# GpSimd drains between experts, result rows scaled on one engine, and the fallback path placed out of line

## Chip, cores and metric

One core of a Trainium2 chip runs the kernel. The metric is the device time of one execution in microseconds (us), as the median of several executions. A profiled execution of the same program gives the rows below; its span is the time from its first to its last instruction.

The engines are TensorE (PE; PEld is its weight load), VectorE (DVE), ScalarE (ACT), GpSimd (POOL) and SyncE (SP). In the rows a name with a q behind it (POOLq, ACTq, PEldq) is the sequencer of that engine: branches, drains, semaphore waits and register loads, which the profile does not count as busy time.

## The reference

A gated linear attention (a state per head that decays by a gate and takes in k times v) gives 3072 rows of 384 numbers. A mixture of 8 experts follows: every row goes to one expert, chosen by the largest gate logit, and comes back scaled.

```python
for t in range(S):                       # S = 768, head_dim 48, 4 x 8 heads
    state = f[:, :, t, :, None] * state + np.einsum('bhd,bhe->bhde', k[:, :, t], v[:, :, t])
    y[:, :, t] = np.einsum('bhd,bhde->bhe', q[:, :, t], state)
...
x = np.ascontiguousarray(attn_out.transpose(0, 2, 1, 3)).reshape(B * S, H * D)
...
e_idx = np.argmax(logits, axis=1)
for e in range(E):                       # E = 8, D = 384, F = 1024
    mask = e_idx == e
    h = np.maximum(x[mask] @ w1[e], 0.0)
    ye = h @ w2[e]
    out[mask] = gate_w[mask, None] * eom[mask, e, None] * ye
```

## The kernel before

The kernel is a program for the Tile framework, fully unrolled. Its first part, until about 127 us of the span, is the attention, in 24 tiles of 128 positions; each tile's rows are scattered by an indirect DMA that POOL issues (line 339, 24 of them) into a DRAM buffer sorted by expert. The second part, `Experts.run`, takes the experts `s` = 0 to 7 in the order of their load; `CAPS` is the number of rows that each may hold (512, 448, 432, 416, 400, 400, 384, 376). Every fp32 product is made of three products of rounded halves (`wh`/`wl`, `hh`/`hl`, `xh`/`xl`).

One expert runs as follows. `mm1` (line 760) makes the hidden tiles `h_ps`, ACT and DVE turn them into `hh` and `hl`. For experts with four row tiles (`s` 0 to 5), `mm2` (line 782) makes the result transposed; `y_out` copies it, and in the next expert's `mm1` stage `put` transposes it back, ACT scales it by the gate (line 820, 384 columns at once) and `scatter` (line 825) sends it to the output rows. For the last two experts (`s` 6 and 7, three row tiles) `mm2_rows` (line 796) makes result rows directly in PSUM: for each row tile, ACT scales the left 192 columns (line 801), DVE the right 192 (line 803), and `scatter` follows.

`scatter` is an indirect DMA that POOL issues. It writes rows of `out`, and each waits for the landing of the one ahead of it, since they write the same tensor. The tile `o` that it reads has three buffers. Apart from the scatters, POOL does only one small conversion per expert in this part (`dst`, line 687).

The order on DVE, ACT, POOL and PE is the order of the code: `chain` fixes it after recording. SP issues the loads of the weights and of the experts' rows, and waits only for free buffers.

At the end, every engine loads a flag (line 1085). If it is set (line 1090), the `general_path` recomputes everything in loops that hold for any input. With these inputs it never is. The program is a list of blocks: the main block, which ends in a conditional branch on each engine; the blocks of the general path; a short block for the case that the flag is not set, in which each engine waits for its own last work; and the end block, in which SP waits for all DMAs, every engine drains and all meet at a barrier, the semaphores are cleared, and all meet once more (rows of line 1130).

Of the kernel before, what the change touches and what calls it, by code (L numbers as in the profile page):

```python
# [13 lines left out]
AF = mybir.ActivationFunctionType  # L14
ALU = mybir.AluOpType
# [5 lines left out]
N, DM, E, F = B * S, H * D, 8, 1024  # L21
# [555 lines left out]
class Experts:  # L577
# [208 lines left out]
    def mm2_rows(self, s, step):  # L786

        k, nc = self.k, self.nc
        for j, n in self.rows(s):
            ps = self.psy.tile([128, 512], F32, name=f"y_ps{j}")  # L790
            i = 0
            for f in range(KF):
                wh, wl = self.whl[2, s, f // 2]
                hh, hl = (t[:, j * TS:j * TS + n] for t in self.hs[s, f][0])
                for a, b in ((hh, wh), (hl, wh), (hh, wl)):
                    nc.tensor.matmul(ps[0:n, 0:DM], a, b[:, f % 2, :], start=(i == 0), stop=(i == 3 * KF - 1))  # L796
                    i += 1
                step(j * KF + f)
            t = self.yp.tile([TS, DM], F32, name="o", bufs=3)
            half = DM // 2  # L800
            nc.scalar.activation(out=t[0:n, 0:half], in_=ps[0:n, 0:half], func=AF.Copy,
                                 scale=k.gain[0:n, j, s:s + 1])
            nc.vector.tensor_scalar(out=t[0:n, half:DM], in0=ps[0:n, half:DM], scalar1=k.gain[0:n, j, s:s + 1],
                                    scalar2=None, op0=ALU.mult)
            self.scatter(s, j, n, t)

    def y_out(self, s):
# [52 lines left out]
    def step(self, n):  # L860
        for _ in range(min(n, len(self.todo))):
            self.todo.pop(0)()

    def run(self):
        step = self.step
        step(len(self.todo))
        self.load_rest(1)
        for f in range(AHEAD):
            if f == AHEAD - 2:
                self.x_late()  # L870
            self.mm2(0, f)
        for s in range(E):
            if s > 0 and s + 1 < E:
                self.load(s + 1, self.k.number[0:1, s + 1:s + 2])
            back = self.rows(s - 1) if s > 0 and len(self.rows(s - 1)) > KC else []
            if s == 0:
                later = self.meta.pop()
                self.gains()
                self.meta = [later]
            for f in range(KF):  # L880
                self.mm1(s, f)
                if s == 0:
                    self.gain(2)
                    if f in (3, 5):
                        self.split(1, 1, f // 2 - 1)
                if f % 2 == 0 and (2, s, f // 2) in self.wr:
                    self.split(2, s, f // 2, self.nc.gpsimd if s == 0 else None)
                if 1 <= f <= len(back):
                    self.put(s - 1, *back[f - 1])
            front = [lambda i=i: self.split(1, s + 1, i) for i in range(KF // 2)  # L890
                     if (1, s + 1, i) in self.wr]
            for c in range(KC):
                front.insert(2 * c + 2 if s > 0 else 2 * c + 1, lambda c=c: self.x_in(s + 1, c))
            if s + 1 == E:
                front = []
            self.gain(len(self.gq))
            self.gains()
            if len(self.rows(s)) <= KC:
                self.mm2_rows(s, lambda i: self.gain(1) if i % 3 != 1 else front.pop(0)() if front else None)
                self.gain(len(self.gq))  # L900
                continue
            for f in range(KF):
                for part in range(len(self.hs[s, f])):
                    if not (s == 0 and part == 0 and f < AHEAD):
                        self.mm2(s, f, part)
                if front:
                    front.pop(0)()
                self.gain(2)
                if s == 1:
                    step(1)  # L910
            self.gain(len(self.gq))
            self.y_out(s)
            if s == 0:
                self.todo += check(self.nc, self.k, self.r, self.kp, self.pso)


def check(nc, k, r, pool, psum):


    ok = pool.tile([128, NTC * NP], F32, name="ok")  # L920
    okc = pool.tile([128, 1], F32, name="okc")
    okb = pool.tile([128, 1], BF16, name="okb")
    bad = pool.tile([128, 1 + 2 * E], F32, name="bad")
    k.bad = pool.tile([128, 1], I32, name="badi")

    def count():
        ps = psum.tile([128, KC, 128], F32, name="o_ps")[:, 0, 0:1]
        nc.tensor.matmul(ps, k.ones, okb, start=True, stop=True)
        nc.vector.tensor_scalar(out=bad[:, 0:1], in0=ps, scalar1=float(128 * NTC * NP), scalar2=None, op0=ALU.is_lt)

    def verdict():
        with nc.allow_low_precision(reason="a count of at most 17"):
            nc.vector.tensor_reduce(out=k.bad, in_=bad, axis=AX.X, op=ALU.add)

    return [
        lambda: nc.vector.tensor_scalar(out=ok, in0=r.pend, scalar1=PMIN, scalar2=None,
                                        op0=ALU.is_ge),
        lambda: nc.vector.tensor_reduce(out=okc, in_=ok, axis=AX.X, op=ALU.add),
        lambda: nc.vector.tensor_copy(out=okb, in_=okc),
        lambda: nc.vector.tensor_tensor(out=bad[:, 1:1 + E], in0=k.tokens, in1=k.caps, op=ALU.is_gt),  # L940
        lambda: nc.vector.tensor_scalar(out=bad[:, 1 + E:1 + 2 * E], in0=k.tokens, scalar1=float(HELD), scalar2=None,
                                        op0=ALU.is_lt),
        count,
        verdict,
    ]
# [107 lines left out]
def chain(tc, nc, engines, start=0):  # L1053

    last = {}
    for i in list(nc.cur_bb.bb.instructions)[start:]:
        if i.engine in engines:
            if i.engine in last:
                tc.add_manual_dep(i, last[i.engine].name,
                                  mybir.DependencyInfo(mybir.DependencyClass.NoSync, mybir.DependencyReason.DATA),  # L1060
                                  reason="order")
            last[i.engine] = i


@with_exitstack
def tile_kernel(ctx: ExitStack, tc: tile.TileContext, q01, k01, f01, q23, k23, f23, v, vT, wg, wgn, w1, w2, out):
    nc = tc.nc
    dram = ctx.enter_context(tc.tile_pool(name="dram", bufs=1, space=DRAM))
    xs_dram = dram.tile([E * N, RW], F32, name="xs_dram")
    y_dram = dram.tile([H, D, N], F32, name="y_dram")  # L1070
    kp = ctx.enter_context(tc.tile_pool(name="const", bufs=1))
    with ExitStack() as cx:
        raw = cx.enter_context(tc.tile_pool(name="raw", bufs=KF // 2))
        r = Routing(kp)
        rt = cx.enter_context(tc.tile_pool(name="rt", bufs=2))
        k = Consts()
        right = cx.enter_context(ExitStack())
        ex = Experts(tc, nc, k, r, raw, right, w1, w2, xs_dram, out, kp)
        with ExitStack() as c1:
            attention(c1, tc, nc, k, kp, rt, q01, k01, f01, q23, k23, f23, v, wg, xs_dram, r, ex)  # L1080
        with ExitStack() as c1:
            ex.open_rest(c1)
            ex.run()
    chain(tc, nc, {getattr(mybir.EngineType, e) for e in ("DVE", "Activation", "Pool", "PE")})
    bad = nc.values_load(k.bad[0:1, 0:1], min_val=0, max_val=1 + 2 * E)

    def part(first, rest):
        return lambda b, h: first[b, h // 2, 64 * (h % 2):64 * (h % 2) + D, :] if b < 2 else rest[b - 2, h]

    with tc.If(bad > 0):  # L1090
        general_path(tc, nc, part(q01, q23), part(k01, k23), part(f01, f23), vT, wgn, w1, w2, y_dram, out)


# [40 lines left out]
```

## Time and profile before

| | us |
|---|---|
| median of 3 executions | 382.46 (382.41 to 382.51) |
| the profiled execution | 382.55 |
| its span | 380.84 |
| TensorE busy | 361.7 (95% of the span) |
| DVE, ACT, POOL busy | 234.8, 196.8, 146.7 |

The profiled execution is 0.09 us over the median, and 1.71 us of it lie outside its span. Shares of busy time are an average over the attention and the expert part.

### The profile page before, as it was taken

The numbers are of one execution on the slowest core, as the hardware profiler recorded it, in microseconds if no ns is written. First come the engines' busy times: TensorE is split into PE (matmuls) and PEld (weight loads), VectorE is DVE, ScalarE is ACT, GpSimd is POOL, SyncE is SP. The second block draws the span as 40 slices with busy tenths as digits, with TensorE's granted clock in tenths as the row PEclk, the third lists the DMA queues.
The fourth block names the chain that finished last, engine by engine and source line by source line (L and its number), as shares of the span: only waits on it lengthen the run. The fifth ranks groups of instructions, "written<-read, shape, count | busy, mean of one in ns | idle before, by whom it ended". The sixth has DMA issues, their size and how long they took to land.

```text
span 380.8 us, 8463 instructions
## 1 busy us (share of the span) xinstructions
PE 361.7 (95%) x3199; PEld 334.2 (88%) x3199; DVE 234.8 (62%) x488; ACT 196.8 (52%) x468; POOL 146.7 (39%) x176
## 2 busy tenths in 40 slices
PE   7899999999998999999999999999999999999990
PEld 2688988898986999899989999999999999999980
DVE  6988989898974655645535545644653654665410
ACT  3576866866756434446336435625634644744310
POOL 6686698999988630002102201301210211231021
PEclk9999999999999999999999999999999999999996
DMA  8999999999178149545453543545444454420010
GB/s 253 348 359 359 312 252 267 299 269 284 47 244 265 54 148 335 177 133 167 134 170 124 175 126 126 167 127 185 133 162 135 159 166 128 160 66 35 2 43 21
DMA packets 51843, 67.75 MB, mean 178 GB/s; under 512 B 3906, under 2 KB 46421, under 8 KB 51792
## 3 DMA queue, kind: packets, MB, share of 16 engines
q1 hardware_dynamic: 48480, 57.46, 50.6%
q0 software_dynamic: 3312, 9.65, 7.0%
q8 instruction: 27, 0.44, 0.5%
q14 instruction: 24, 0.20, 0.2%
HBM read 54.16 MB, written 13.39 MB: 177 GB/s over the span
## 4 chain that ended last, share of the span: by engine, by line
PE 78%; DVE 9%; ACT 3%; issue 3%; DMA 3%; POOL 2%; POOLq 0%; DVEq 0%; ACTq 0%
PE h_ps L760 28%; PE y_ps L782 22%; PE x_ps L322 5%; PE y_ps L796 4%; PE a_ps L245 3%; PE x_ps L710 3%; PE two_ps L309 2%; DVE p L209 2%; DVE i L216 2%; PE o_ps L817 2%; PE two_ps L305 2%; PE one_ps L309 2%; PE kn_ps L262 2%; PE one_ps L278 2%; DMA out<-o,dst 2%
## 5 line engine op out<-in xcount | busy, mean ns | idle before, releaser
L825 POOL DMA_INDIRECT out<-o,dst x30 | 31.7, 1058 | 187.8 <-ACT o L820 118.6
L765 DVE SCALAR_TENSOR_TENSOR hl<-h_ps,hh 128x256 fp32r<-128x256 f32 (+6 forms) x72 | 39.3, 547 | 51.2 <-ACT hh L764 50.8
L760 PE MATMUL h_ps<-xh,w1h 128*128 128x400 f32 (+6 forms) x192 | 67.4, 351 | 0.3 <-DVE hl L765 0.3
L760 PE MATMUL h_ps<-xh,w1l 128*128 128x400 f32 (+6 forms) x192 | 65.0, 338 | 0.0
L760 PE MATMUL h_ps<-xl,w1h 128*128 128x400 f32 (+6 forms) x192 | 65.0, 338 | 0.0
L764 ACT ACTIVATE hh<-h_ps 128x256 fp32r<-128x256 f32 (+6 forms) x72 | 34.8, 484 | 50.1 <-PE h_ps L760 48.5
L782 PE MATMUL y_ps<-hh,w2h 128*128 128x256 f32 (+4 forms) x168 | 57.7, 343 | 0.0
L782 PE MATMUL y_ps<-hl,w2h 128*128 128x256 f32 (+4 forms) x168 | 55.7, 331 | 0.0
L782 PE MATMUL y_ps<-hh,w2l 128*128 128x256 f32 (+4 forms) x168 | 55.6, 331 | 0.0
L717 DVE TENSOR_TENSOR xl<-x_ps,xh 128x400 fp32r<-128x400 f32 (+6 forms) x23 | 13.1, 569 | 41.8 <-ACT xh L716 38.4
L760 PEld LDWEIGHTS h_ps<-xh,w1h 128*128 128x128 f32 x192 | 36.1, 188 | 1.2 <-DVE hl L765 0.6
L716 ACT CAST xh<-x_ps 128x400 fp32r<-128x400 f32 (+6 forms) x23 | 11.3, 490 | 48.9 <-PE x_ps L710 42.3
L760 PEld LDWEIGHTS h_ps<-xl,w1h 128*128 128x128 f32 x192 | 36.1, 188 | 0.4
L760 PEld LDWEIGHTS h_ps<-xh,w1l 128*128 128x128 f32 x192 | 36.0, 188 | 0.5
L636 DVE TENSOR_TENSOR w2l<-w2r,w2h 128x768 fp32r<-128x768 f32 x31 | 30.7, 989 | 4.2 <-ACT w2h L635 1.3
L223 POOL TENSOR_TENSOR q_t<-q_t,p 128x512 f32<-128x512 f32 x24 | 30.6, 1276 | 6.1 <-DVE p L209 5.9
L245 PE MATMUL a_ps<-q_t,k_t 64*128 64x128 f32 x384 | 28.4, 285 | 4.5 <-DVE k_t L220 2.7
L782 PEld LDWEIGHTS y_ps<-hh,w2h 128*128 128x128 f32 x168 | 31.6, 188 | 1.1
L782 PEld LDWEIGHTS y_ps<-hl,w2h 128*128 128x128 f32 x168 | 31.6, 188 | 0.5
L782 PEld LDWEIGHTS y_ps<-hh,w2l 128*128 128x128 f32 x168 | 31.7, 189 | 0.4
L209 DVE TENSOR_TENSOR_SCAN p<-f_ps,start_p 128x511 f32<-128x511 f32 x22 | 28.0, 1274 | 4.0 <-ACT start_p L197 2.4
L245 PEld LDWEIGHTS a_ps<-q_t,k_t 64*128 64x128 f32 x384 | 23.7, 187 | 7.1 <-POOL q_t L223 2.0
(176 smaller groups left out, 773.4 us busy)
## 6 DMA issues: line engine op xcount, KB each, us to landing
w1r<-in_w SPq DMA_DIRECT2D x32, 384.0 KB, 3.7
w2r<-in_w SPq DMA_DIRECT2D x32, 384.0 KB, 3.2
v_t<-in_v SPq DMA_DIRECT2D x12, 512.0 KB, 8.6
xg<-xs_dram SPq DMA_DIRECT2D x5, 802.0 KB, 5.0
xs_dram<-empty SPq DMA_DIRECT2D x8, 401.0 KB, 10.9
f_t<-in_f SPq DMA_DIRECT2D x6, 512.0 KB
q_t<-in_q SPq DMA_DIRECT2D x6, 512.0 KB, 9.4
k_t<-in_k SPq DMA_DIRECT2D x6, 512.0 KB, 8.6
```

The costliest lines, as they stand in the source:

```text
L209: nc.vector.tensor_tensor_scan(out=flat(d["p"])[:, 1:n], data0=flat(d["f"])[:, 0:n - 1], data1=sp[:, 1:n], initial=sp[:, 0:1], op0=ALU.mul ...
L223: nc.gpsimd.tensor_tensor(out=q_t[i][:, :, sl], in0=q_t[i][:, :, sl], in1=d["p"], op=ALU.mult)
L245: nc.tensor.matmul(aps[t][par][:, g, :], k_t[b % 2][r, g, sl], q_t[b % 2][r, g, sl], start=(g == 0), stop=(g == NP - 1))
L309: nc.tensor.matmul(yps[t][g % 2][r0:r0 + 64, g // 2, :], v_t[b][:, c, 64 * h:64 * h + 64], at[t][:, h % 2, g, :], start=(c == 0 and h < 4) ...
L322: nc.tensor.matmul(xps[t][:, g, :], xt[t][:, g, :], turn[:, g, :], start=(g == 0), stop=(g == NP - 1))
L636: (eng or self.nc.vector).tensor_tensor(out=flat(lo), in0=flat(t), in1=flat(hi.bitcast(F32)), op=ALU.subtract)
L760: nc.tensor.matmul(ps[:, 0:n], a[:, c, cs], b, start=(i == 0), stop=(i == 3 * KC - 1))
L764: nc.scalar.activation(out=hi, in_=ps[:, 0:n], func=AF.Relu)
L765: nc.vector.scalar_tensor_tensor(out=lo, in0=ps[:, 0:n], scalar=0.0, in1=hi.bitcast(F32), op0=ALU.max, op1=ALU.subtract)
L782: self.nc.tensor.matmul(self.ys[d][:, c0:c0 + n], a[:, f % 2, ds], b, start=(f == 0 and i == 0 and part == 0), stop=(f == KF - 1 and i == ...
L796: nc.tensor.matmul(ps[0:n, 0:DM], a, b[:, f % 2, :], start=(i == 0), stop=(i == 3 * KF - 1))
L825: self.nc.gpsimd.indirect_dma_start(out=self.out, out_offset=bass.IndirectOffsetOnAxis(ap=self.k.dst[0:n, j, s:s + 1], axis=0), in_=t[0:n] ...
```

## The change

Three things are changed.

- At the start of experts 2 to 7, after the loads of the next expert are issued on SP, POOL executes a `drain`. In POOL's queue each drain stands behind the `dst` conversion of that expert and ahead of the scatters of the expert before; the one of expert 7 stands behind the three scatters of expert 6 and ahead of those of expert 7. The drains are not listed in the order rows below, which leave drains out.
- In `mm2_rows`, ACT scales all 384 columns of a result row tile, and DVE does nothing there (six row tiles in all).
- The branch on the flag prefers to go on to the block of the case that the flag is not set. That block now stands directly behind the main block; the general path and then the end block follow it.

```diff
@@ mm2_rows
             t = self.yp.tile([TS, DM], F32, name="o", bufs=3)
-            half = DM // 2
-            nc.scalar.activation(out=t[0:n, 0:half], in_=ps[0:n, 0:half], func=AF.Copy,
-                                 scale=k.gain[0:n, j, s:s + 1])
-            nc.vector.tensor_scalar(out=t[0:n, half:DM], in0=ps[0:n, half:DM], scalar1=k.gain[0:n, j, s:s + 1],
-                                    scalar2=None, op0=ALU.mult)
+            nc.scalar.activation(out=t[0:n], in_=ps[0:n, 0:DM], func=AF.Copy, scale=k.gain[0:n, j, s:s + 1])
             self.scatter(s, j, n, t)
@@ run
         for s in range(E):
             if s > 0 and s + 1 < E:
                 self.load(s + 1, self.k.number[0:1, s + 1:s + 2])
+            if s > 1:
+                self.nc.gpsimd.drain()
             back = self.rows(s - 1) if s > 0 and len(self.rows(s - 1)) > KC else []
@@ tile_kernel
-    with tc.If(bad > 0):
+    with tc.If(bad > 0, preferred_fallthrough_block=False):
         general_path(tc, nc, part(q01, q23), part(k01, k23), part(f01, f23), vT, wgn, w1, w2, y_dram, out)
```

On POOL at the end of the main block, the scatters of experts 6 and 7 stood so before. In brackets are the semaphores that a row waits for: DMASW ones belong to scatters ahead, DVE and Activation to the scaling of the row tile.

```order
L825 DMA out<-o,dst 3072x384 [waits DMASW1_49,DVE_49]
L825 DMA out<-o,dst 3072x384 [waits DMASW2_49,DVE_49,Pool_49]
L825 DMA out<-o,dst 3072x384 [waits DMASW3_49,DVE_49]
L825 DMA out<-o,dst 3072x384 [waits DMASW4_49,DVE_49]
L1085 TENSOR_LOAD badi [waits DVE_49]
L1090 COMPARE_AND_BRANCH
```

And so they stand now.

```order
L821 DMA out<-o,dst 3072x384 [waits DMASW1_49,Activation_49]
L821 DMA out<-o,dst 3072x384 [waits DMASW2_49,Activation_49,Pool_49]
L821 DMA out<-o,dst 3072x384 [waits DMASW3_49,Activation_49]
L821 DMA out<-o,dst 3072x384 [waits DMASW4_49,Activation_49]
L1083 TENSOR_LOAD badi [waits DVE_49]
L1088 COMPARE_AND_BRANCH
L1088 UNCONDITIONAL_BRANCH [waits Pool_49]
```

A scatter now waits for ACT where it waited for DVE. Behind the conditional branch there is an unconditional one to the end block, which waits for POOL's own compute instructions ahead of it; the general path comes after it.

On PE at the same place, the last matmuls of expert 7 and what follows them were these before:

```order
L796 MATMUL y_ps_4893<-w2h,hl 120x384
L796 MATMUL y_ps_4893<-w2l,hh 120x384
L1085 TENSOR_LOAD badi [waits DVE_49]
L1090 COMPARE_AND_BRANCH
L973 COMPARE_AND_BRANCH
```

They are these now:

```order
L796 MATMUL y_ps_4894<-w2h,hl 120x384
L796 MATMUL y_ps_4894<-w2l,hh 120x384
L1083 TENSOR_LOAD badi [waits DVE_49]
L1088 COMPARE_AND_BRANCH
L1088 UNCONDITIONAL_BRANCH [waits PE_49]
L971 COMPARE_AND_BRANCH
```

Before, the conditional branch was the jump over the general path, and the wait for PE's own matmuls came after it. Now the wait for the last matmul comes first, and the jump behind it.

## Rows read from the trace of the kernel before

**Rows 1.** The page: its first line.

```profile
span 380.8 us, 8463 instructions
```

**Rows 2.** Busy time by stretch (us, and instructions), then granted clock and DMA.

```profile
core 0: us, PE busy (x) PEld busy (x) DVE busy (x) ACT busy (x) POOL busy (x), PEclk, DMA share, GB/s
127.00:370.60 243.60, 242.59 (x1447) 232.51 (x1445) 127.11 (x271) 113.88 (x223) 41.55 (x43) 1.00 0.43 137
370.60:380.84 10.24, 0.00 (x0) 0.00 (x0) 0.42 (x1) 0.35 (x1) 1.03 (x1) 0.64 0.07 19
```

**Rows 3.** The chain of waits from 355 us on: start, us, what.

```profile
362.61 0.43 DVE o L803
...
363.80 2.58 DMA out<-o,dst
...
367.53 3.83 DMA out<-o,dst
...
372.48 0.76 POOL out L825
```

**Rows 4.** Line 825 from 372 us on: the landing of the last scatter.

```profile
DMA to landing us min/median/max: 3.0/3.0/3.0
```

**Rows 5.** Line 1090: count, ns min/median/max, first and last start in us.

```profile
L1090 PEldq COMPARE_BRANCH  x1: 3722/3722/3722, 367.8 to 367.8; - x1
L1090 ACTq COMPARE_BRANCH  x1: 50/50/50, 371.1 to 371.1; - x1
...
L1090 POOLq COMPARE_BRANCH  x1: 53/53/53, 372.5 to 372.5; - x1
...
L1090 DVEq EVENT_SEMAPHORE  x1: 21/21/21, 374.9 to 374.9; - x1
L1090 POOLq EVENT_SEMAPHORE  x1: 17/17/17, 375.4 to 375.4; - x1
```

**Rows 6.** Line 1130 (the end block) from 371 to 380.1 us.

```profile
L1130 SPq DRAIN  x2: 7/10/12, 375.9 to 376.0; - x2
...
L1130 ACTq DRAIN  x1: 10/10/10, 374.1 to 374.1; - x1
L1130 POOLq DRAIN  x1: 4492/4492/4492, 375.5 to 375.5; - x1
L1130 DVEq DRAIN  x1: 135/135/135, 377.3 to 377.3; - x1
```

**Rows 7.** Line 1130 from 380.05 us on: what follows POOL's long drain.

```profile
L1130 POOLq EVENT_SEMAPHORE  x4: 17/17/17, 380.1 to 380.7; - x4
...
L1130 POOLq DRAIN  x2: 40/74/107, 380.2 to 380.6; - x2
```

**Rows 8.** Line 1125 (the start of the program): POOL's first drain.

```profile
L1125 POOLq DRAIN  x1: 176/176/176, 0.4 to 0.4; - x1
```

**Rows 9.** POOL's groups by line: the scatters of both parts.

```profile
L825 POOL DMA_INDIRECT out<-o,dst x30 | 31.7, 1058 | 187.8 <-ACT o L820 118.6 <-DVE o L803 28.7 <-ACT hh L764 26.1
...
L339 POOL DMA_INDIRECT xs_dram<-xn,slot x24 | 24.3, 1011 | 7.7 <-issue 3.8 <-DVE misc L292 1.7 <-DVE state L290 1.2
```

**Rows 10.** POOL in order of time; in brackets its idle time ahead.

```profile
322.72 1.09 POOL L825 DMA_INDIRECT out<-o,dst  x1 [15.77 <-ACT o L820]
...
363.80 0.98 POOL L825 DMA_INDIRECT out<-o,dst  x1 [16.12 <-DVE o L803]
...
372.21 1.03 POOL L825 DMA_INDIRECT out<-o,dst  x1 [3.70 <-DVE o L803]
```

**Rows 11.** ACT and DVE in order of time: the last two row tiles.

```profile
366.84 0.42 DVE L803 TENSOR_SCALAR o<-y_ps,gain 128x192 f32<-128x192 f32 x1 [3.82 <-ACT o L801]
370.53 0.42 ACT L801 ACTIVATE o<-y_ps,gain 120x192 f32<-120x192 f32 x1 [3.73 <-PE y_ps L796]
370.99 0.42 DVE L803 TENSOR_SCALAR o<-y_ps,gain 120x192 f32<-120x192 f32 x1 [3.73 <-ACT o L801]
```

**Rows 12.** Line 820: ACT scales 384 columns (ns min/median/max).

```profile
L820 ACT ACTIVATE o<-o_ps,gain x24: 569/578/588, 169.3 to 327.9; 128x384 f32<-128x384 f32 x19, 16x384 f32<-16x384 f32 x2, 64x384 f32<-64x384 f32 x1, 48x384 f32<-48x384 f32 x1
```

**Rows 13.** DMA queues from 367.5 to 371.4 us (packets, MB, share).

```profile
q8 instruction: 1, 0.02, 2.1%
```

## Prediction

> **What bounds the kernel now.** I first read the busy time by stretch. From 127 to 370.60 us, the whole expert part, TensorE is busy 242.59 of 243.60 us at a granted clock of 1.00, and the other engines about half of that or less [rows 2]. So in this stretch an instruction taken from DVE, ACT or POOL is worth nothing by itself; only TensorE's 1.01 us of idle time could be. Behind it lie 10.24 us, from 370.60 to 380.84, without a single matmul [rows 2]. All three edits reach into that tail, so I looked there next.
>
> The chain of waits shows its first half. The three scatters of the last expert run one behind the other: the first is issued at 363.80 and lands after 2.58 us, the second at 367.53 and lands after 3.83 us, the third follows [rows 3] at 372.21 [rows 10], and lands 3.0 us later [rows 4], at 375.2. The chain ends there, with POOL's last instruction at 373.2, and does not tell why the span goes on to 380.84. The rows of the end block do: SP's drains are done by 376.0, ACT's at 374.1, DVE's at 377.4, but POOL starts a drain at 375.5 that takes 4.492 us, to 380.0 [rows 6]. The events of the barrier come at 380.1 and later [rows 7]. From 377.4 to 380.0 all engines wait for that one drain. When it starts, POOL's last instruction has been over for 2.3 us, and the last scatter has landed. So it is not waiting for the work in flight.
>
> **The drains.** What is in 4.492 us? POOL's first drain, at 0.4 us, takes 0.176 us [rows 8]; the two right after the long one take 0.107 and 0.040 [rows 7]. Between the first and the long one POOL has issued 24 + 30 = 54 indirect DMAs [rows 9], whose rows had all landed. I take it that each leaves POOL something to clear at the next drain. That is an inference; an estimate of its size is (4.492 − 0.107) / 54 = 0.081 us for each.
>
> By this estimate the six new drains take: for `s` = 2, behind the 24 scatters of the attention and four of expert 0, 28 x 0.081 + 0.107 = 2.4 us; for `s` = 3 to 6, behind four each, 0.43 us; for `s` = 7, behind four of expert 5 and three of expert 6, 0.67 us. Only the last three scatters are left for the drain at the end: 0.35 us instead of 4.49. The six cost nothing where they stand: behind each in POOL's queue are the scatters of the expert before (for `s` = 7, its own), and POOL is idle for at least 15.77 us ahead of the first of these, 16.12 ahead of the last three [rows 10]. If that cover were gone, the scatters would start up to 2.4 us later, and the three buffers of `o` would come free later for ACT. The bounds of the saving are nothing (a fixed cost of that place) and 4.45 us (0.040 left, the shortest drain); I take 4.14, since the short drains are those with no scatter ahead.
>
> The Trainium skill speaks against that. PSUM — Partial Sum Buffer, section Engine vs sequencer instructions, says that a drain waits for the engine to go fully idle. By it a drain of an engine whose instructions are over has nothing to wait for, earlier drains take nothing off the last, and the time would be that of the first rival below. No rule there allows for 4.49 us behind an idle engine, as [rows 6] have it.
>
> **ACT alone.** A row tile of the last two experts takes from ACT's start at 370.53 to DVE's end at 371.41, 0.88 us, as DVE follows ACT [rows 11]. ACT alone needs 0.578 us for 384 columns [rows 12]: 0.30 less for each. For the first five tiles TensorE goes on and hides it; the bound, if it did not, is ACT's 0.16 us more (0.578 − 0.42) for five, 0.8 us. The last tile is on the path only if its scatter waits for it. It did not: the scatter started at 372.21, 0.80 behind the tile but also 0.85 behind the landing of the second (367.53 + 3.83 = 371.36) [rows 3, 10]. The second started 0.27 behind its tile (366.84 + 0.42 = 367.26) [rows 3, 11], so it moves to 367.24, limited now by the landing of the first as well. Whether the third moves hangs on the second's landing.
>
> **Out of line.** Each engine jumps over the general path before; the end block still stands behind it now, so each engine still jumps, only behind an unconditional branch that waits for the engine's last work. PE's jump takes 3.722 us from 367.8, where the others' own branches take 50 to 53 ns but the next event comes about 3 us later (POOL 372.5 to 375.4) [rows 5]. In that time the DMA queues carry one instruction packet of 0.02 MB [rows 13], and the second scatter takes 3.83 us instead of 2.58 [rows 3]. I take it that PE's fetch delays the scatter: no other row tells the two scatters apart. Now PE waits for its last matmul at 370.5 ahead of the jump. Then the second lands at 367.24 + 2.58 = 369.82, and the third is free to follow its tile: 370.53 + 0.58 + 0.27 = 371.38, which is 0.83 earlier. Bounds: the first scatter came 0.76 behind its tile (363.04) [rows 3], which makes 371.87; and 371.91 (0.30 earlier) if the fetch is not what delayed the second and it still takes 3.83. The jumps are covered: PE 370.5 + 3.7 = 374.3, ACT 371.1 + 3.0 = 374.1; DVE has no work in the last tiles and jumps long before.
>
> The Trainium skill (Runtime: NRT & Kernel Launch, section Instruction fetch mechanics) says that a taken branch to outside the window of two pages forces a fetch before execution can go on. The 2.9 to 3.7 us of [rows 5] agree; by it too the jump stays, because its target is still behind the general path.
>
> **The sum.** The third scatter starts at 371.38. POOL's branch comes 0.3 later as before, at 371.7, its jump takes 2.9, to 374.6, and its drain starts at 374.7 and ends at 375.05. The third scatter lands at 371.38 + 3.0 = 374.4; SP's drains came 0.8 behind the landing, now 375.2. That is the later of the two, so SP's wait is what is late next. The barriers took 380.84 − 379.99 = 0.85, so the span is 376.05, which is 4.8 less, of which the drain's 4.14 are the larger part. The profiled execution was 382.55 for its span of 380.84 [rows 1, 2], so 377.76, and the median lies 0.09 below: **377.7 us**. Its own range is 377.0 (a shorter barrier, shorter landings) to 378.6 (a third scatter bound at 371.9, and 0.4 of jump or drain).
>
> **The rivals.** *The last drain does not shrink.* It is the cost of that place or of that code, not of the scatters. For it: no drain with scatters ahead of it but this one is in the trace. Against it: the two drains of the same block are short [rows 7]. POOL's drain then ends at 374.7 + 4.49 = 379.2, which makes 381.6 (382.15 if the third scatter gains only 0.30).
>
> *It shrinks by half,* since only some of the scatters, or the oldest, can be cleared early: 374.7 + 2.25 = 376.95, and 379.5.
>
> *The end code of an engine crosses a page.* Six more instructions stand on POOL, and blocks have moved on all. DVE took 2.4 us from its event at 374.9 to its drain at 377.3 [rows 5, 6], and other engines had less, so such a stall is there, hidden. On POOL behind its jump it would give 375.05 + 2.4 + 0.85 = 378.3, and 379.9.
>
> *Slower: the 4.49 us is a fetch, not scatter work.* PE's branch shows that a stall can lie in an instruction's own duration (3.722 us for what takes ACT 0.050) [rows 5]. Then the drains save nothing, and with the code moved POOL may meet one stall of 2.4 more between its jump and the barrier: 380.84 − 0.83 + 2.4 = 382.4, and 384.0. It decides once the new stall is over 0.83 + 0.76 = 1.6 us. Against it: the drain is the third or fourth instruction behind a jump that had just fetched its target.
>
> *Edit three does nothing:* the second scatter still takes 3.83. That makes 378.2, within my range.
>
> **How the numbers follow.** A measurement of this kernel tells about 0.2%, 0.76 us, from no change. Chances: my forecast, with the last case in it, 0.79; no shrinking 0.08 (its times, 381.6 to 382.15, lie at the edge of 0.2% and within; I count 0.07 of it as the same and 0.01 as faster); half 0.05; the page 0.04; slower 0.04. Faster is 0.79 + 0.05 + 0.04 + 0.01 = 0.89, the same 0.07, slower 0.04. The range of 377.0 to 380.0 holds the forecast, the half and the page; what it leaves out has 0.12.
>
> **What the profile after would show.** On POOL, drains of about 2.4, then four of 0.43, then 0.67 us, and one of at most 0.5 in the end block. If the first takes 2.4 and the last 0.35, the count of scatters is what sets them; if all are near 0.1 and the last near 4.5, it is a fixed cost; if the last is short and the first too, something else cleared it. Six rows of ACT at 578 ns with 384 columns, and none of DVE. The second scatter landing after 2.6 us with no instruction packet beside it, and the third starting at 371.4. A short conditional branch on PE and its unconditional one behind 370.5. A span of 376.0. What would make me wrong: a last drain over 2 us, or SP or another engine late at the barrier by a stall that no row shows yet.

## Result and the profile after

The changed kernel takes **377.73 us** (median of 4, 377.69 to 377.84) where the kernel before, measured beside it, took 382.44: a ratio of 0.9874, interval 0.9856 to 0.9893. The forecast was 377.7.

The span and its tail, the page's first line and then the busy time by stretch (columns as in [rows 2]):

```profile
span 376.0 us, 8457 instructions
```

```profile
core 0: us, PE busy (x) PEld busy (x) DVE busy (x) ACT busy (x) POOL busy (x), PEclk, DMA share, GB/s
127.00:370.60 243.60, 242.29 (x1444) 232.24 (x1442) 124.99 (x266) 114.62 (x222) 40.76 (x43) 1.00 0.43 137
370.60:376.10 5.50, 0.00 (x0) 0.00 (x0) 0.00 (x0) 0.27 (x1) 1.03 (x1) 0.93 0.13 34
```

The expert part is what it was: TensorE is busy 242.29 us against 242.59. By these stretches the whole difference lies behind 370.60, where no matmul runs: 10.24 us before and 5.4 now (to the span's end at 376.0). The end block, line 1128 now, shows why (count, ns min/median/max, first and last start; compare [rows 6, 7]):

```profile
L1128 POOLq DRAIN  x3: 46/107/393, 374.6 to 375.7; - x3
L1128 SPq DRAIN  x3: 7/7/13, 375.1 to 375.4; - x3
L1128 ACTq DRAIN  x2: 8/54/100, 373.6 to 375.4; - x2
L1128 PEldq DRAIN  x2: 8/40/72, 374.3 to 375.5; - x2
L1128 DVEq DRAIN  x1: 10/10/10, 375.4 to 375.4; - x1
...
L1128 DVEq DRAIN  x1: 58/58/58, 362.0 to 362.0; - x1
```

POOL's drain of 4.492 us has become one of 0.393. It ends at 375.0, and SP comes to its drains at 375.1, so the two are now late together; DVE reached its first drain long before, at 362.0 (the last row, from an earlier window). The chain of waits shows the other half (start, us, what; compare [rows 3]):

```profile
361.86 0.59 ACT o L800
...
363.22 3.50 DMA out<-o,dst
...
367.51 2.59 DMA out<-o,dst
...
371.42 0.79 POOL out L821
```

The second scatter lands after 2.59 us instead of 3.83, and the third starts at 371.18 instead of 372.21. But the first takes 3.50 instead of 2.58. From 367.5 to 370.1 us, beside the second scatter, the DMA queues carry the scatter's own packets and no instruction packet:

```profile
q0 software_dynamic: 64, 0.20, 20.4%
```

The branch on the flag, line 1088 (compare [rows 5]):

```profile
L1088 DVEq COMPARE_BRANCH  x2: 51/53/55, 358.7 to 358.9; - x2
L1088 PEldq COMPARE_BRANCH  x2: 95/1964/3833, 367.5 to 370.4; - x2
L1088 ACTq COMPARE_BRANCH  x2: 38/44/49, 370.8 to 371.0; - x2
L1088 POOLq COMPARE_BRANCH  x2: 41/44/48, 371.5 to 371.7; - x2
```

Each engine has two branches now. PE's first falls through in 95 ns at 367.5; the jump, 3.833 us, comes at 370.4 behind its last matmul. DVE jumps at 358.9, 12.7 us earlier than before.

The six new drains, line 872: all of them, and the first and the last alone.

```profile
L872 POOLq DRAIN  x6: 3025/4318/5029, 181.6 to 345.9; - x6
...
L872 POOLq DRAIN  x1: 5029/5029/5029, 181.6 to 181.6; - x1
...
L872 POOLq DRAIN  x1: 3025/3025/3025, 345.9 to 345.9; - x1
```

They take 3.0 to 5.0 us, not 0.43 to 2.4. Each starts while the scatter ahead of it is only being issued, and ends behind its landing. The scatter ahead of the last of them starts at 346.10 and lands 2.5 us later, at 348.6; the drain ends at 348.9. The four in the middle also end 0.2 us behind the landing of their scatter. The first of the six, which follows 28 scatters, ends later against its own, at 186.7, 1.2 us behind the landing at 185.5. These are the scatter ahead of it, that scatter's landing, and POOL's next instruction:

```profile
181.81 0.97 POOL L821 DMA_INDIRECT out<-o,dst  x1 [2.75 <-ACT hh L764]
...
DMA to landing us min/median/max: 3.7/3.7/3.7
...
182.81 0.27 POOL L687 TENSOR_SCALAR dst<-xg 128x4 int32<-128x4 f32 x1
```

### The profile page after: what moved, and what is told of

The parts are those of the page before. It is cut to its first block, busy times and chain, and to the rows that moved or that the text cites. A ratio compares the mean times of both kernels' runs of the same rounds, so it can differ in the third digit from the quotient of the medians.

```text
span 376.0 us, 8457 instructions
## 1 busy us (share of the span) xinstructions
PE 362.4 (96%) x3199; PEld 334.4 (89%) x3199; DVE 232.4 (62%) x482; ACT 197.9 (53%) x468; POOL 145.9 (39%) x176
## 4 chain that ended last, share of the span: by engine, by line
PE 79%; DVE 9%; ACT 3%; issue 3%; DMA 3%; POOL 1%; POOLq 0%; DVEq 0%; ACTq 0%
PE h_ps L760 28%; PE y_ps L782 23%; PE x_ps L322 5%; PE y_ps L796 5%; PE a_ps L245 3%; PE x_ps L710 3%; PE two_ps L309 3%; DVE p L209 2%; DVE i L216 2%; PE o_ps L813 2%; PE two_ps L305 2%; PE one_ps L309 2%; PE kn_ps L262 2%; PE one_ps L278 2%; DMA out<-o,dst 2%
## 5 line engine op out<-in xcount | busy, mean ns | idle before, releaser
L636 DVE TENSOR_TENSOR w1l<-w1r,w1h 128x768 fp32r<-128x768 f32 x28 | 26.7, 955 | 4.4 <-ACT w1h L635 3.5
```

The source lines that it names most:

```text
L636: (eng or self.nc.vector).tensor_tensor(out=flat(lo), in0=flat(t), in1=flat(hi.bitcast(F32)), op=ALU.subtract)
```

## Experiments

Each is compared with the kernel before, measured beside it, which took 382.0 to 382.1 us there. "One run" means one time only.

**Drains alone.** The kernel before, with only these lines added:

```diff
+            if s > 1:
+                self.nc.gpsimd.drain()
```

> The kernel before with the six drains alone. What the traces of before and after show: POOL's last drain went from 4.492 to 0.393 us. If POOL alone held the end, the span would be shorter by about 4.1 us (378.3 us of time). But in the trace of before DVE's own drain came only at 377.3, behind its last row tile and a jump, and with the old scaling and the old place of the blocks it should be as late here: then the barrier waits for DVE, the span is about 377.45 + 0.85 = 378.3 and the time about 379.9. My theory is 379.9; the rival, that the drains carry the whole gain by themselves, says 378.3 or less.

Measured: 379.50 us, ratio 0.9932 (0.9915 to 0.9948). The drains alone give 2.5 of the 4.7 us. The end block (line 1132 there):

```profile
L1132 POOLq DRAIN  x3: 46/107/296, 375.1 to 377.3; - x3
L1132 SPq DRAIN  x3: 7/7/13, 375.6 to 377.0; - x3
...
L1132 DVEq DRAIN  x2: 10/72/134, 376.6 to 377.0; - x2
```

POOL is through at 375.4 and SP at 375.7, but DVE only comes to its drain at 376.6. The wait has moved from POOL to DVE.

**No drains.** The changed kernel without the two lines.

> The changed kernel without the six drains. Theory (each scatter leaves POOL something to clear): the last drain takes 4.4 to 4.5 us again behind 54 scatters; it starts at 374.6 as in the changed kernel and ends at 379.1, span 379.9 to 380.0, time 381.6. Rival (the long drain is a property of the old place of the end block, such as a fetch): the last drain is 0.4 to 2.4 us though no drain came earlier, and the time 377.7 to 379.7.

Measured: 381.44 us, ratio 0.9985 (0.9976 to 0.9995).

```profile
L1126 POOLq DRAIN  x3: 40/107/4562, 374.4 to 379.6; - x3
```

With the end block where the change puts it, the drain is as long as ever. So the 4.5 us do not belong to the old place.

**One drain, at expert 7 or at expert 2.** `if s > 1` becomes `if s == 7`, or `if s == 2`.

> The changed kernel with one drain only, that of expert 7. Theory, 0.081 us for each scatter since the last drain, counted from the landing of the scatter ahead: the one drain stands behind 51 scatters and ends some 4.2 us behind that landing; the last one stands behind three and takes 0.39 us as with six drains; time 377.7. Rival, a slope of about 0.04 us (28 scatters took 1.55 us behind their landing in the changed kernel): the one drain ends some 2.3 us behind the landing; the last is the same, and so is the time. Rival, that one drain cannot clear what six clear: a last drain over 1 us and a time over 378.3.

> The changed kernel with one drain only, that of expert 2, so that 26 scatters are left for the last drain. Theory, 0.081 us for each: 0.107 + 26 x 0.081 = 2.2 us, end of the drain at 376.8, time 379.4. Rival, a slope of 0.04 us with 2 us that only the old last drain had: 1.2 to 1.3 us, time 378.5. Rival, that any earlier drain makes the last one short: 0.4 us and 377.7.

Measured, one run each: 377.32 and 379.09 us. With the drain at expert 7, that one (line 872) and those of the end block:

```profile
L872 POOLq DRAIN  x1: 5463/5463/5463, 345.7 to 345.7; - x1
...
L1128 POOLq DRAIN  x3: 46/107/372, 374.2 to 375.3; - x3
```

With the drain at expert 2, those of the end block:

```profile
L1128 POOLq DRAIN  x3: 46/107/2261, 374.2 to 377.0; - x3
```

Three scatters leave 0.37 us (0.30 to 0.39 in the kernels with six drains), 26 leave 2.26, 54 leave 4.56 (no drains). From 3 to 26 that is 0.082 us for each, from 26 to 54 also 0.082. The forecast of 0.081 holds over the whole length, for scatters that have all landed. With one still in flight, neither theory of the drain at expert 7 fits: it ends at 351.2, 2.7 us behind the landing at 348.5, where they said 4.2 and 2.3. It ends 4.2 us behind POOL's last instruction, at 346.9, which is what 51 scatters cost (51 x 0.081 + 0.107). That would fit a drain that clears what has landed while it waits for the rest. But the drain at expert 2 does not bear it out: it ends 3.6 us behind POOL's last instruction in the changed kernel (186.7 for 183.1), where 28 scatters cost 2.4. How the clearing goes together with the wait for a landing stays open. (The 1.55 us that the expectation gives for these 28 are counted from the scatter's last packet, at 185.1, not from its landing.)

**Fewer scatters, and half the rows.** Both without drains. What they leave out stands in the expectations.

```diff
     def scatter(self, s, j, n, t):
+        if s < 6:                        # first kernel
+            return
+        n = min(n, 64) if s < 6 else n   # second kernel
```

> The changed kernel without drains, and without the 24 scatters of experts 0 to 5, whose result rows are left out of the output; all other work of POOL stays. 30 scatters are left for the last drain. Theory, 0.081 us for each: 0.107 + 30 x 0.081 = 2.54 us, time about 379.6. Rival, that the drain clears something of POOL's other instructions, or has a fixed cost: 4.5 us as without drains, 381.4.

> The changed kernel without drains, in which the scatters of experts 0 to 5 send at most 64 rows each, the other rows being left out of the output: 54 scatters as before, but 5224 rows instead of 6440. If the last drain counts scatters it takes 4.5 us; if it counts rows, 0.107 + 4.4 x 0.81 = 3.7 us, and the time is 0.8 less than the 381.4 of the kernel without drains.

Measured, one run each: 379.50 and 381.59 us. With 30 scatters:

```profile
L1128 POOLq DRAIN  x3: 40/107/2602, 374.3 to 377.5; - x3
```

With 54 scatters and four fifths of the rows:

```profile
L1127 POOLq DRAIN  x3: 40/107/4573, 374.4 to 379.5; - x3
```

The count of scatters sets the drain, not the rows that they send, and not POOL's other instructions, which were all there in the first of the two.

**Halves back.** The changed kernel with the old scaling.

```diff
-            nc.scalar.activation(out=t[0:n], in_=ps[0:n, 0:DM], func=AF.Copy, scale=k.gain[0:n, j, s:s + 1])
+            half = DM // 2
+            nc.scalar.activation(out=t[0:n, 0:half], in_=ps[0:n, 0:half], func=AF.Copy,
+                                 scale=k.gain[0:n, j, s:s + 1])
+            nc.vector.tensor_scalar(out=t[0:n, half:DM], in0=ps[0:n, half:DM], scalar1=k.gain[0:n, j, s:s + 1],
+                                    scalar2=None, op0=ALU.mult)
```

> The changed kernel with the old scaling of result rows (ACT and DVE a half each). With the drains alone, DVE's drain at 376.6 was the last to reach the barrier, 2.5 us behind the event that followed its jump. Theory A: DVE is late because it still has work in the last row tile; then its drain comes at 374.1 + 2.5 = 376.6 here too and the time is about 379.2. Theory B: the stall belongs to the old place of the blocks; then only the 0.30 us of the last row tile come back (third scatter at 371.5) and the time is about 378.0.

Measured: 379.79 us, ratio 0.9938 (0.9925 to 0.9952).

```profile
L1132 POOLq DRAIN  x3: 46/107/393, 374.7 to 376.0; - x3
...
L1132 DVEq DRAIN  x2: 10/34/58, 374.7 to 377.8; - x2
L1132 DVEq EVENT_SEMAPHORE  x2: 21/21/21, 377.7 to 378.0; - x2
```

POOL has gone through all its drains by 376.0. DVE's first drain is at 374.7, but its next instruction, the event of the barrier, comes at 377.7, and all wait for it. The time is nearer to theory A (379.2) than to B (378.0); the stall sits one instruction later than A said.

**Only the last row tile on ACT alone.**

```diff
-            half = DM // 2
+            half = DM if (s, j) == (7, 2) else DM // 2
...
+            if half < DM:
```

> The changed kernel in which only the very last row tile is scaled by ACT alone; the five before it have a half on DVE again. Theory: with the halves back DVE lost 2.0 us because its end code, 3 us of jump and 2.5 to 2.9 us of a second stall, began only behind the last row tile at 371.4. Here DVE is through with its work at 367.2 and with both stalls at about 373, ahead of SP's 375.1; the time is that of the changed kernel, 377.7, or up to 0.3 more where DVE's fetches lie beside the second scatter. Rival: all six row tiles matter (ACT alone frees something in the stages before), then between 378 and 379.8.

Measured: 377.48 us, ratio 0.9896 (0.9868 to 0.9925), the same as the changed kernel within the intervals. Five of the six times lie from 377.37 to 377.54; the sixth is 381.0, and nothing here says why.

```profile
L1133 DVEq DRAIN  x2: 10/34/57, 370.3 to 375.2; - x2
L1133 DVEq EVENT_SEMAPHORE  x2: 21/21/21, 375.1 to 375.7; - x2
```

DVE still scales five halves, but not the last, reaches its drain at 370.3, and its event comes with the barrier at 375.1. Of the six row tiles one matters, and it matters because DVE comes to its drain 4.4 us earlier than with the halves back (370.3 for 374.7).

**DVE's end code moved.** The kernel with the halves back, and 16 instructions more on DVE:

```diff
+            if s == 7:
+                pad = self.kp.tile([128, 1], F32, name="pad")
+                for _ in range(16):
+                    self.nc.vector.memset(pad, 0.0)
```

> The kernel with the halves back and, in addition, 16 small memsets of a tile that nothing reads on DVE in the first part of expert 7, which move DVE's end code by 16 instructions. If DVE's stall of 2.9 us between its first drain and the next event is the edge of an instruction page in its end code, it goes away and the time is about 377.9 to 378.1. Rival: the stall follows DVE's jump wherever the code stands (17 instructions fewer on DVE had not moved it); then DVE's event stays some 2.9 us behind its drain and the time near 379.8.

Measured: 378.27 us, ratio 0.9900 (0.9886 to 0.9914).

```profile
L1136 POOLq DRAIN  x3: 46/107/393, 375.0 to 376.2; - x3
...
L1136 DVEq DRAIN  x2: 10/34/58, 374.9 to 375.9; - x2
L1136 DVEq EVENT_SEMAPHORE  x2: 21/21/21, 375.8 to 376.4; - x2
```

DVE is as late as with the halves back (374.9), but the event follows with the barrier at 375.8 and not 2.9 us behind the drain. More instructions made the kernel 1.5 us faster. That speaks for an edge in the instruction stream. It doesn't settle it: before, with the drains alone and with the old place, the stall stood ahead of DVE's drain, although in the last of these DVE has 17 instructions fewer.

**Old place of the general path.** The changed kernel with `tc.If(bad > 0)` as before.

> The changed kernel with the general path back in its old place (drains and scaling by ACT as changed). Theory: PE's jump lies beside the second scatter again, which takes 3.8 to 3.9 us; the third starts at about 371.75 instead of 371.18 and the time is about 378.1, 0.4 more than the changed kernel; DVE, which has nothing in the last row tiles, reaches the barrier early. Rival: DVE's stall hangs on the place of the blocks and not on its work, then its drain is at 376 or later and the time is 379 or more. Rival: the fetch does not slow the scatter, then 377.7.

Measured: 378.34 us, ratio 0.9909 (0.9894 to 0.9924). The DMA queues during the second scatter there (packets, MB, share, and the scatter's us to landing):

```profile
q0 software_dynamic: 64, 0.20, 13.7%
q8 instruction: 1, 0.02, 2.1%
...
out<-o,dst POOLq DMA_INDIRECT x1, 4.0
```

The instruction packet and the slow landing are back together. Putting the path out of line is worth 0.6 us between the medians, 1.0 between the differences from the kernel before measured beside each (3.74 and 4.71); the third scatter starts 0.7 us later here, at 371.9. That holds with DVE out of the way. With the halves on DVE it is worth nothing: 379.79 us out of line (halves back), 379.50 in the old place (drains alone). No run has this edit by itself.

**ACT alone.** The kernel before with ACT scaling the whole row, nothing else.

> The kernel before with the scaling by ACT alone. Theory: POOL's drain of 4.5 us stays the last, and only the scatters move: the second is issued 0.3 us earlier, beside PE's fetch as before, and so the third; about 0.3 us less than before. DVE reaches the barrier early, but nothing waits for it. Rival: freeing DVE is worth 2 us by itself, then 380.

Measured: 382.16 us (381.48 to 382.68), ratio 1.0005 (0.9995 to 1.0014): no change. POOL's drain takes 4.492 us and is last, as the theory said; the 0.3 us don't show. In its chain of waits (of the execution with 381.48, the fastest) the first scatter takes 3.66 us and the second 3.08:

```profile
362.98 3.66 DMA out<-o,dst
...
367.41 3.08 DMA out<-o,dst
```

The first one is slower than in [rows 3]. DVE, free early, jumps at 358.5; three instruction packets follow, at 359.5, 362.2 and 364.6, and the third lies beside this scatter.

**One drain more, ahead of the last scatter.**

```diff
     def scatter(self, s, j, n, t):
+        if s == 7 and j == 2:
+            self.nc.gpsimd.drain()
```

> The changed kernel with one drain more, directly ahead of the last scatter, where nothing covers it. Theory: a drain behind a scatter in flight ends 0.55 to 0.7 us behind its landing; the second scatter lands at 370.1, so this one ends at 370.7 or so, and the third scatter, whose own issue takes 0.75 us behind what it waits for, starts at about 371.5 instead of 371.2; the last drain falls from 0.39 to about 0.2 us, but SP waits for the landing. Time 377.9 to 378.1. Rival: the drain costs as little here as elsewhere, and the shorter last drain makes it 377.5 to 377.7.

Measured: 378.47 us, ratio 0.9907 (0.9892 to 0.9921). The time is 0.4 over the forecast, but not in the way that the theory said. The new drain, POOL's third scatter and its landing:

```profile
L822 POOLq DRAIN  x1: 2932/2932/2932, 366.9 to 366.9; - x1
...
L823 POOL DMA_INDIRECT out<-o,dst x1: 1026/1026/1026, 371.0 to 371.0; - x1
...
DMA to landing us min/median/max: 4.0/4.0/4.0
```

The drain ends at 369.8 and holds nobody up: the third scatter starts at 371.0, even a little earlier than in the changed kernel. The last drain, behind one scatter, takes 0.190 us, as forecast. But the third scatter lands after 4.0 us, not 3.2. More instruction packets lie beside it here (six from 371.0 to 375.2, where the changed kernel has four up to the landing); whether a drain so late causes that, no run tells.

## Why the prediction was right, step by step

**The long drain.** Right, and the largest term. The last drain was to be 0.35 us and is 0.393. The rate of 0.081 us per scatter was inferred from one row divided by a count; 1, 3, 26, 30 and 54 scatters now lie on that line within 0.07 us. The first rival (a fixed cost of the place) and the slower one (a fetch) fall with the kernel without drains, the rival of one half with the drain at expert 7. (The sums of two of these rivals are off by 0.1 us: they give 381.7 where the prediction has 381.6, and 379.4 where it has 379.5. Nothing hangs on it.) The Trainium skill's rule that the prediction sets against it (PSUM — Partial Sum Buffer, section Engine vs sequencer instructions: a drain waits for the engine to go fully idle) says too little here. The drains in the middle wait on, past POOL's last instruction (347.1), for the landing of the scatter in flight (348.6), and behind 54 landed scatters the wait is 4.5 us.

**The six drains.** Their lengths were mis-sized: 2.4, 0.43 and 0.67 us against 5.0, 3.8 to 5.0, and 3.0. The step counted only the clearing; the drain stands directly behind a scatter and also waits for that to land. It cost nothing, because the cover was 15.77 us [rows 10], and no scatter of POOL starts later than it did (322.44 for 322.72; the 30 of the expert part are 0.03 to 1.04 us earlier).

**ACT alone.** The row takes 0.58 to 0.59 us as forecast, and the five earlier ones are hidden. But the step valued the edit at 0.30 us, as a part of the third scatter's start. That part is right (371.46 with the halves back, 371.18 now), but in the changed kernel the edit is worth 2.1 to 2.4 us (379.79 against 377.73, or the differences from the kernel before measured beside each: 2.29 against 4.71). The prediction had DVE's 2.4 us from event to drain in [rows 5, 6], and said in half a sentence that DVE "jumps long before"; it did not say what the sum would be if DVE did not. With only POOL's drain gone, DVE at 377.4 would have been next, as the drains alone show. The sum came out right because it took DVE to be early, which this edit brings about; what each edit is worth did not come out. Taken out of the changed kernel one at a time, the drains cost 3.7 us (381.44), the scaling on ACT 2.1 (379.79) and the place 0.6 (378.34). That is 6.4 for a change of 4.7, because POOL's late end and DVE's lie side by side: either one, back by itself, holds up the barrier.

**Out of line.** Right in its way: PE's jump is behind 370.4, the second scatter lands after 2.59 us, and in every kernel in which no instruction packet lay beside it (no drains, halves back) it took 2.6. The third starts at 371.18, forecast 371.38: the last matmuls ended 0.3 us earlier. That lead is luck and not the change: the first scatter of the expert part already has it (170.35 for 170.66), ahead of the first drain. The third landed after 3.2 us instead of 3.0, and so the two small misses cancel. The second started at 367.51 instead of 367.24, because the first now took 3.50. An instruction packet lies there too (from 363.2 to 366.7 us):

```profile
q0 software_dynamic: 64, 0.20, 15.5%
q14 instruction: 1, 0.01, 0.7%
```

It is the third of three (359.9, 362.6, 365.4); the first comes 1.0 us behind DVE's jump, and no other engine jumps in that time, so I take them for DVE's. In the kernel with the halves back, where DVE jumps at 371.6, no such packet lies there and the first scatter takes 2.6 us. So the two edits seem to work against each other a little: the one takes the packet behind PE's jump away from the second scatter, the other puts one of DVE's beside the first.

**The end.** SP 375.1 (forecast 375.2), the barriers 0.85, the span 376.0 (376.05). SP is what is late now: from the third landing at 374.4 to its drain it runs eleven semaphore instructions, 0.06 us apart.

## What to carry to other kernels

When an engine is late at the end, write down when each of the others arrives, too: taking away 4.1 us from POOL alone gave 2.5, since DVE was next. A drain of GpSimd behind many indirect DMAs costs time for each of them (0.08 us here), and an earlier drain in a stretch where GpSimd is idle pays that in advance; in one run a single late one did as much as six. Take the last piece of work away from an engine whose end code stalls, rather than look for the fastest split of that piece.

## What the runs showed of the hardware that was not expected

- A drain on GpSimd waits for the landing of an indirect DMA in flight: behind four scatters or seven it ended 0.2 to 0.3 us behind the landing, behind 28 1.2 us, behind 51 2.7 us.
- DVE stalled 2.3 to 2.9 us among the first instructions of its end code, behind a jump that had already taken about 3 us. 16 instructions more on DVE took the stall away (379.79 to 378.27 us).
- Instruction packets of 8 to 16 KB beside a scatter go with a landing of 2.8 to 4.0 us among the last three scatters, where it takes 2.6 without.
